# Threshold attention and gMLP on one core: transposes of two chunks at a time, loads one per step, value blocks in plain order

## The chip, the cores and the metric

The kernel runs on one core of one Trainium2 chip. Time is device microseconds (us) of one execution; several runs of one kernel are given by their median. The engines are PE (matrix multiply), DVE (vector), ACT (activation functions), POOL (GpSimd) and SP (here only an issuer of DMAs); each works through its own instructions in program order.

## What is computed

Attention with a threshold over 8 batches of 8 heads, 576 positions and 64 columns per head, and behind it a gMLP (spatial gating unit) on the joined heads.

```python
scores = (1/8) * q @ k.T
scores = where(scores >= max(scores) - tau, scores, -1e9)       # per row
attn   = exp(scores - max) ; attn /= sum(attn)
x      = (attn @ v)            # heads joined: (8, 576, 512)
h      = relu(x @ w_in)        # (8, 576, 1024)
u, v   = h[..., :512], h[..., 512:]
v_n    = (v - mean(v)) / sqrt(var(v) + 1e-6)
v_s    = einsum('ts,bsd->btd', w_spatial, v_n) + b_spatial[:, None]
out    = (u * v_s) @ w_out     # (8, 576, 512)
```

## The kernel before

Two heads of one batch are a pair; the 32 pairs are 32 slots of five steps. Step `c` of a slot takes one chunk of queries: chunks 0 to 3 are 128 queries of each of the two heads against 576 keys (1152 columns), chunk 4 is the last 64 queries of both heads. A step (`step`, L446 on) does this: PE computes the scores into one of two PSUM tiles `s` of three banks (L415, L418), DVE takes the row maximum `negm` (L460), ACT the exponential `e` (L468). One step later `mask` (L429) lets DVE set to zero what is under the threshold and write bf16 (`p`, L434; `pr` for chunk 4, L440), and SP issues a DMA that transposes the result SBUF to SBUF (`pT`, L437; `ptr` in two halves, L443 and L444), since the product with the values wants the keys on the partitions. That product, `pv` (L232), runs one slot later: head 0 of slot i in step 3 of slot i+1, head 1 in step 4. PE goes through chunk 0, 1, 2, 3 (from `pT`) and then chunk 4 (from `ptr`) in 25 small matmuls (L245), DVE normalises (`r`, `xn`, L254 and L255), and after head 1 one more DMA transpose makes `xT` (L260).

The work of the gMLP is cut into 20 jobs for each batch: five each of `moe_v`, `moe_u`, `moe_s`, `moe_o`. One is laid into each step, 27 steps behind the attention. So the `moe_v` jobs of a batch stand in steps 2, 3, 4 of slots 5, 9, 13, ... 29 and in steps 0, 1 of the slot after it, `moe_u` in the next five steps, and so on; each fourth slot has the same work. A `moe_v` job ends in a norm: ACT writes `vrel` with its sum (L297), POOL makes `nmean` of it (L299), ACT the squares `sq` (L305), POOL in turn `rs` (two instructions), `nm` and `vn` (L307 to L311). These jobs and `pv` share two PSUM banks `f`. For the last batch, which runs when the attention is over, the norm is made by DVE instead (L287 to L293), with one POOL instruction in it, and `uT` by DVE (L339).

In steps 0, 1, 2 of a slot PE also transposes q and k of the next pair (`qk_main`, `qk_rem`). What they read was loaded some slots ahead: in step 0 of every odd slot up to 27, SP issues nine loads for two pairs (L111 and L114 for q and k, L122 to L129 for v), all in one place, and POOL reshapes them (`shape_v` in step 0, L155; `shape_qk` in step 1, L146 and L149). The order on each engine is the order in which the program is written. At the start of slot 0, in step 3, `load_weights` issues the weights, the spatial matrix `wsl` from SP.

The lines that set the place of the loads, and of the first transposes behind them:

```python
                if c == 1 and slot + 2 < NPAIR:
                    shape_qk(slot + 2)
                if c == 0:
                    shape_v(slot)
                if c == 0 and slot % 2 and slot + 3 < NPAIR:
                    load_qk(slot + 3, 2)
                    load_v(slot + 3)
            ...
            step(i, c, fs[0] if fs else None, fs[1] if len(fs) > 1 else None)
```

Of the kernel before, what the change touches and what calls it, by code (L numbers as in the profile page):

```python
# [17 lines left out]
def kernel(  # L18
# [16 lines left out]

# [7 lines left out]
    P = 128  # L43
# [23 lines left out]
    NP_ = 3  # L67
    p_ring = [const.tile([P, 1152], BF16, name=f"p{i}") for i in range(NP_)]
    pr_ring = [const.tile([P, 704], BF16, name=f"pr{i}") for i in range(2)]
    v_ring = [const.tile([P, 10, D + 1], BF16, name=f"v{i}") for i in range(4)]  # L70
# [29 lines left out]
    wsl = const.tile([P, 5, S], F32, name="wsl")  # L100
    brow = const.tile([1, S], F32, name="brow")

    def load_qk(i, n):

        b, hp = divmod(i, HP)
        for t, src in zip(ld_ring[i // 2 % 2], (q, k)):
            t = t[:, 2 * (i % 2):2 * (i % 2) + 2 * n]
            src = src[b, 2 * hp:2 * hp + 2 * n]  # L110
# [6 lines left out]
    def load_v(i):  # L117
        b, hp = divmod(i, HP)
        vv = ld_ring[i // 2 % 2][2].rearrange("p (j h) c d -> p j (h c) d", h=2)
        va = v[b, 2 * hp:2 * hp + 4].rearrange("(j h) s d -> h j s d", h=2)  # L120
        fold = "j (p c) d -> p j (c d)"
        nc.sync.dma_start(out=vv[:, :, 0:4, :], in_=va[0, :, 0:512, :].rearrange(fold, c=4))  # L122
        nc.sync.dma_start(out=vv[0:64, :, 4, :],
                          in_=va[0, :, 512:576, :].rearrange("j p d -> p j d"))
# [4 lines left out]
        nc.sync.dma_start(out=vv[64:128, :, 9, :],  # L129
                          in_=va[1, :, 512:576, :].rearrange("j p d -> p j d"))  # L130
# [22 lines left out]
    def shape_v(i):  # L153
        j = i % 2
        nc.gpsimd.tensor_copy(  # L155
            out=v_ring[i % 4][:, :, 0:D],
            in_=ld_ring[i // 2 % 2][2][:, 2 * j:2 * j + 2].rearrange("p h c d -> p (h c) d"))


    def load_weights():  # L160
# [9 lines left out]
        nc.sync.dma_start(out=wsl[:, 0:4, :],  # L170
                          in_=moe_w_spatial[0:512, :].rearrange("(p c) s -> p c s", c=4))
        nc.sync.dma_start(out=wsl[0:64, 4, :], in_=moe_w_spatial[512:576, :])

    def shape_ws(c):
        n = P if c < 4 else 64
        nc.gpsimd.tensor_copy(
            out=wsb[:n, c, 0:512].rearrange("p (sc sp) -> p sc sp", sc=4),
            in_=wsl[:n, c, 0:512].rearrange("p (sp sc) -> p sc sp", sc=4))
        nc.gpsimd.tensor_copy(out=wsb[:n, c, 512:576], in_=wsl[:n, c, 512:576])
        nc.sync.dma_start_transpose(out=wsT[:, :, c * P:(c + 1) * P], in_=wsb[:, c, :])  # L180

    def shape_bias():
# [9 lines left out]
        nc.gpsimd.tensor_tensor(out=r2, in0=r1, in1=mid, op=ALU.subtract)
        nc.gpsimd.tensor_copy(out=lo, in_=r2)
        for n, t in enumerate((hi, mid, lo)):
            nc.sync.dma_start(out=wsT[64 + n:65 + n, 4, 0:S], in_=t[0:1, :])
# [367 lines left out]
```

## Time and profile before

| | |
|---|---|
| three runs | 627.15, 624.07, 620.58 us; median 624.07 |
| the profiled execution | 627.79 us |
| its span, first to last instruction | 625.7 us |
| PE matmul busy | 502.8 us (80% of the span) |
| DVE busy | 471.1 us (75%) |
| ACT, POOL busy | 327.9 us (52%), 223.1 us (36%) |
| SP's DMA queue, share of 16 DMA engines | 69.5% |
| mean granted TensorE clock | 0.918 |

Busy time counts every instruction from start to end, and neighbours on PE and DVE overlap a little, so an engine that shows 97% in a stretch is full there. The profile names for each engine what ended its idle times (the waits), follows back the chain of work that ended last, and gives for each DMA the time from issue to landing. The timeline gives start and length of each instruction; a bracket at its end is the idle time of its engine before it and what ended it.

### The profile page before, as it was taken

Reading aid. Unit: us, or ns where it says so; the run is one execution under the profiler, and the core shown is the slowest. Engines: PE = TensorE matmul, PEld = TensorE weight load, DVE = VectorE, ACT = ScalarE, POOL = GpSimd, SP = SyncE. Lnnn points to the kernel's source line nnn. Section 1 sums busy time; section 2 is a strip of 40 time slices with the busy share of each in tenths; the row PEclk is TensorE's granted clock in tenths of the full one; section 3 lists DMA queues with packets and bytes.
Section 4 is the critical chain, followed back from the end, with each engine's and each line's share of the span. In section 5 each row is a group of like instructions: output and inputs, shape, how many; then the busy total and the mean of one; then the engine's idle time right before and its main releaser. Section 6 shows DMA issues by size and latency. Waiting matters only on the chain.

```text
span 625.7 us, 10432 instructions
## 1 busy us (share of the span) xinstructions
PE 502.8 (80%) x3790; PEld 264.4 (42%) x3840; DVE 471.1 (75%) x516; ACT 327.9 (52%) x605; POOL 223.1 (36%) x398
## 2 busy tenths in 40 slices
PE   4725758688998989787997879787997879979756
PEld 2313334344544445343554435444554435535323
DVE  0835869788996879687896879677895869969463
ACT  1612435575475636575376726675375735765211
POOL 6527212373215522373116522364115622261010
PEclk9976879899997989899898989899897979989979
DMA  7799696948597687968698676957697585835502
GB/s 199 121 192 198 120 196 112 200 82 192 92 232 135 123 171 147 191 115 182 91 214 151 126 158 152 207 93 169 113 208 154 93 182 78 193 73 104 145 1 75
DMA packets 244930, 90.41 MB, mean 145 GB/s; under 512 B 214480, under 2 KB 239568, under 8 KB 244752
## 3 DMA queue, kind: packets, MB, share of 16 engines
q1 hardware_dynamic: 243744, 88.17, 69.5%
q0 software_dynamic: 1136, 1.58, 1.7%
q8 instruction: 30, 0.49, 0.3%
q14 instruction: 20, 0.16, 0.1%
HBM read 32.79 MB, written 9.44 MB: 67 GB/s over the span
## 4 chain that ended last, share of the span: by engine, by line
PE 36%; DVE 23%; DMA 15%; issue 8%; POOL 7%; ACT 6%; SPq 4%; POOLq 0%; ACTq 0%; DVEq 0%
PE s L415 14%; DVE p L434 10%; DVE negm L460 9%; DMA ptr<-pr 8%; PE f L245 6%; PE f L358 5%; DMA kl<-in_k_dram 3%; DMA wsl<-in_moe_w_spatial_dram 3%; PE f L324 2%; PE f L275 2%; ACT e L468 2%; ACT sq L305 2%; PE s L418 2%; PE f L388 2%; PE f L208 2%
## 5 line engine op out<-in xcount | busy, mean ns | idle before, releaser
L468 ACT ACTIVATE e<-s,negm 128x576 f32<-128x576 f32 x288 | 199.5, 739 | 135.7 <-DVE negm L460 127.7
L460 DVE TENSOR_REDUCE negm<-s 128x2 f32<-128x1152 f32 (+1 forms) x160 | 197.3, 1233 | 60.8 <-PE s L415 60.0
L434 DVE SCALAR_TENSOR_TENSOR p<-e,ctau 128x1152 bf16<-128x1152 f32 x128 | 189.2, 1478 | 13.2 <-DMA pT<-p 11.7
L415 PE MATMUL s<-qkT 64*128 64x512 f32 (+1 forms) x768 | 198.1, 611 | 1.2 <-ACT e L468 1.0
L229 POOL COPY kd<-qkT 64x64 f32<-64x64 f32 x32 | 7.4, 231 | 243.9 <-ACT qkT L225 224.0
L415 PEld LDWEIGHTS s<-qkT 64*128 64x128 f32 (+1 forms) x768 | 58.2, 181 | 35.1 <-issue 12.5
L212 ACT COPY qkT<-f 128x512 f32<-128x512 f32 x64 | 37.5, 586 | 63.8 <-PE f L208 63.8
L245 PEld LDWEIGHTS <-pT 128*128 128x128 bf16 x1280 | 51.6, 103 | 45.5 <-issue 23.1
L245 PE MATMUL f<-v,ptr 128*128 128x65 bf16 x320 | 22.7, 207 | 59.0 <-DMA ptr<-pr 59.0
L245 PE MATMUL f<-v,pT 128*128 128x65 bf16 x1280 | 56.2, 201 | 15.0 <-DMA pT<-p 10.4
L418 PE MATMUL s<-kd,qkT 128*128 128x128 f32 x256 | 55.8, 301 | 9.2 <-ACT e L468 6.9
L418 PEld LDWEIGHTS s<-kd,qkT 128*128 128x128 f32 x256 | 45.3, 197 | 25.0 <-ACT e L468 8.3
L254 DVE RECIPROCAL r<-f 128x5 f32<-128x5 f32 x64 | 12.2, 190 | 56.6 <-PE f L245 56.1
L146 POOL TENSOR_SCALAR qn<-ql 128x640 f32<-128x640 f32 x32 | 47.7, 1489 | 3.0 <-DMA ql<-in_q_dram 2.8
L275 PE MATMUL f<-w_in,xT 128*128 128x512 bf16 x145 | 43.8, 408 | 4.5 <-issue 1.3
L358 PE MATMUL f<-wsT,vn 128*128 128x512 bf16 x145 | 44.6, 429 | 2.9 <-ACT uT L344 1.0
L324 PE MATMUL f<-xT,w_in 128*128 128x512 bf16 x121 | 34.1, 396 | 13.0 <-ACT vrel L297 5.6
L388 PE MATMUL f<-w_o,gT 128*128 128x512 bf16 (+1 forms) x147 | 40.0, 379 | 2.7 <-DVE gT L375 1.3
L245 PEld LDWEIGHTS <-ptr 128*128 128x128 bf16 x320 | 16.1, 105 | 60.6 <-DMA ptr<-pr 56.0
L297 ACT ACTIVATE vrel<-f 128x512 f32<-128x512 f32 x35 | 20.8, 595 | 29.7 <-PE f L275 29.3
L396 ACT COPY o<-f 128x512 f32<-128x512 f32 (+1 forms) x38 | 22.2, 583 | 24.1 <-PE f L388 22.3
L255 DVE TENSOR_TENSOR xn<-f,r 128x320 bf16<-128x320 f32 x64 | 31.5, 491 | 2.2
(76 smaller groups left out, 489.3 us busy)
## 6 DMA issues: line engine op xcount, KB each, us to landing
out_dram<-o SPq DMA_DIRECT2D x32, 256.0 KB, 2.9
ql<-in_q_dram SPq DMA_DIRECT2D x15, 512.0 KB, 4.6
kl<-in_k_dram SPq DMA_DIRECT2D x15, 512.0 KB, 5.6
vl<-in_v_dram SPq DMA_DIRECT2D x16, 256.0 KB, 5.7
vl<-in_v_dram SPq DMA_DIRECT2D x32, 128.0 KB, 4.8
pT<-p SPq DMA_TRANSPOSE x128, 3.3
wsl<-in_moe_w_spatial_dram SPq DMA_DIRECT2D x1, 1152.0 KB, 18.3
vl<-in_v_dram SPq DMA_DIRECT2D x32, 32.0 KB, 4.9
```

What stands on the lines that cost most here:

```text
L146: nc.gpsimd.tensor_scalar(out=t, in0=src, scalar1=scale, scalar2=0.0, op0=ALU.mult, op1=ALU.add)
L212: nc.scalar.copy(out=qks[i][:, which, 0:512], in_=hold["t"])
L245: nc.tensor.matmul(out=t[:, c * 65:c * 65 + 65], lhsT=pts[i, c][:, blk, lo:lo + P], rhs=vt[:, 5 * h + j, :], start=(j == 0), stop=(j == 4))
L275: nc.tensor.matmul(out=t, lhsT=xts[b][:, f, c * P:(c + 1) * P], rhs=w_in[:, f, 512:1024], start=(f == 0), stop=(f == 3))
L324: nc.tensor.matmul(out=t, lhsT=w_in[:, m, f * P:(f + 1) * P], rhs=xts[b][:, m, 0:512], start=(m == 0), stop=(m == 3))
L358: nc.tensor.matmul(out=t, lhsT=vn[:, c, f * P:(f + 1) * P], rhs=wsT[:, c, 0:512], start=(c == 0), stop=(c == 4))
L388: nc.tensor.matmul(out=t[:n], lhsT=gs[b][:, f, c * P:c * P + n], rhs=w_o[:, f, :], start=(f == 0), stop=(f == 3))
L415: return nc.tensor.matmul(out=out, lhsT=qk[hs, 0, m], rhs=qk[hs, 1, lo:lo + n], start=True, stop=True)
L418: nc.tensor.matmul(out=view(s, 512, [[448, 2], [1, 64]]), lhsT=qk[:, 0, c * P:(c + 1) * P], rhs=kd_ring[i % 2], start=True, stop=True)
L434: nc.vector.scalar_tensor_tensor(out=pt, in0=ef, scalar=ctau, in1=ef, op0=ALU.is_ge, op1=ALU.mult)
L460: nc.vector.tensor_reduce(out=nm[:, 0:nh], in_=s, axis=AX.X, op=ALU.max, negate=True)
L468: nc.scalar.activation(out=e[:, h, :], in_=s[:, h, :], func=ACT.Exp, bias=nm[:, h:h + 1])
```

## The change

- `mask` writes chunks 0 and 1 into one tile, 2 and 3 into another, and issues one DMA transpose for each two chunks (18 blocks of 128x128, before 9); chunk 4 is transposed by one DMA of 5 blocks instead of two of 5 half blocks. `pv` indexes the new tiles. The value blocks of head 1 stay in plain order, with one extra block `vx` for the last 64 positions, which has its own small load and POOL copy (L147 of the changed kernel).
- The loads go into a queue, seven for two pairs (v in three instead of five), and one of them is issued at the head of each step; two per step in the first five.
- `shape_qk` stands in step 2 instead of step 1.
- `wsl` is loaded in three parts into tiles that the gMLP uses later.
- When the scores are over, the gMLP's jobs take their PSUM bank in turn from the two banks `f` and from the two score tiles. `uT` of the last batch is made by ACT. Its norm is put on the list `later`.

```diff
+    def load(i, n, w):
...
+        t = ld_ring[i // 2 % 2][w][:, 2 * (i % 2):2 * (i % 2) + 2 * n]
+        src = (q, k, v)[w][b, 2 * hp:2 * hp + 2 * n]
+        def main():
             nc.sync.dma_start(
                 out=t[:, :, 0:4, :],
                 in_=src[:, 0:512, :].rearrange("h (p c) d -> p h (c d)", c=4))
+        def rest():
             nc.sync.dma_start(out=t[0:64, :, 4, :],
                               in_=src[:, 512:576, :].rearrange("h p d -> p h d"))
...
+        def rest_b():
+            nc.sync.dma_start(
+                out=vx_ring[i // 2 % 2][64:128],
+                in_=src.rearrange("(j h) s d -> h s j d", h=2)[1, 512:576])
+        return [main, rest] + ([rest_b] if w == 2 else [])
...
+    def bank():
+        banks[0] += 1
+        if "scores" in done_with and banks[0] % 2:
+            return ps_s.tile([P, 1536], F32, name="s")[:, 0:512]
+        return ps_f.tile([P, 512], F32, name="f")
...
                 for j in range(5):
-                    blk = 4 + j if (h == 1 and c < 4) else j
-                    lo = 64 if (h == 1 and c == 4) else 0
...
+                    if c < 4:
+                        lhs = pts[i, c // 2][:, c % 2, 4 + (j + 1) % 5 if h else j, :]
+                        rhs = vt[:, (10 if j == 4 else 5 + j) if h else j, :]
+                    else:
+                        lhs = pts[i, 2][:, j, 64 * h:64 * h + P]
+                        rhs = vt[:, 5 * h + j, :]
...
                 nc.gpsimd.tensor_tensor(out=rs, in0=rs, in1=mhalf, op=ALU.pow)
-                nc.vector.tensor_scalar(out=dst, in0=vrel[:n], scalar1=mv[:n, 0:1],
-                                        scalar2=rs[:n], op0=ALU.subtract, op1=ALU.mult)
+                def norm():
+                    nc.vector.tensor_scalar(out=dst, in0=vrel[:n], scalar1=mv[:n, 0:1],
+                                            scalar2=rs[:n], op0=ALU.subtract, op1=ALU.mult)
+                later.append(norm)
...
-            if f < 4 and b == B - 1:
-                nc.vector.tensor_scalar(out=us[b][:, f, 0:512], in0=t, scalar1=0.0, scalar2=0.0,
-                                        op0=ALU.max, op1=ALU.add)
-            elif f < 4:
+            if f < 4:
                 nc.scalar.activation(out=us[b][:, f, 0:512], in_=t, func=ACT.Relu)
...
-            pt = p_ring[(i * 4 + c) % NP_]
+            pt = p_ring[c // 2]
...
-            dst = ptp.tile([P, 9, P], BF16, name="pT")
-            nc.sync.dma_start_transpose(out=dst, in_=pt)
+            if c % 2:
+                dst = ptp.tile([P, 2, 9, P], BF16, name="pT")
+                nc.sync.dma_start_transpose(out=dst.rearrange("p c b s -> p (c b) s"),
+                                            in_=pt.rearrange("p c s -> p (c s)"))
+                pts[i, c // 2] = dst
...
-            dst = ptr_ring[i % 3]
-            nc.sync.dma_start_transpose(out=dst[:, :, 0:64], in_=pt[0:64, 64:704])
-            nc.sync.dma_start_transpose(out=dst[:, :, 64:128], in_=pt[64:128, 0:640])
+            pts[i, 2] = ptr_ring[i % 3]
+            nc.sync.dma_start_transpose(out=pts[i, 2][:, :, 0:P], in_=pt)
...
-                if c == 1 and slot + 2 < NPAIR:
+                if c == 2 and slot + 2 < NPAIR:
                     shape_qk(slot + 2)
...
-                if c == 0 and slot % 2 and slot + 3 < NPAIR:
-                    load_qk(slot + 3, 2)
-                    load_v(slot + 3)
+                if c == 0 and slot % 2 and slot + 3 < NPAIR or g == 0:
+                    for w in range(3):
+                        queue.extend(load(slot + (3 if g else 2), 2, w))
...
+            else:
+                done_with.add("scores")
...
+            for f in queue[:1 if g > 4 else 2]:
+                queue.pop(0)()
             step(i, c, fs[0] if fs else None, fs[1] if len(fs) > 1 else None)
```

SP, around step 0 of an odd slot in the steady part: `xT` of the slot before closes step 4 of the even slot, then come the odd slot's loads and `ptr`. Before:

```order
L437 DMA_TRANSPOSE pT<-p_104 128x9x128
L260 DMA_TRANSPOSE xT<-xn 128x5x128
L111 DMA ql_116<-in_q_dram 128x4x256
L114 DMA ql_116<-in_q_dram 64x4x64
L111 DMA kl_117<-in_k_dram 128x4x256
L114 DMA kl_117<-in_k_dram 64x4x64
L122 DMA vl_118<-in_v_dram 128x2x256
L123 DMA vl_118<-in_v_dram 64x2x64
L125 DMA vl_118<-in_v_dram 64x2x256
L127 DMA vl_118<-in_v_dram 64x2x256
```

Behind these stand the ninth load and then the two halves of `ptr`. Of the change:

```order
L438 DMA_TRANSPOSE pT<-p_103 128x18x128
L264 DMA_TRANSPOSE xT<-xn 128x5x128
L107 DMA ql_115<-in_q_dram 128x4x256
L446 DMA_TRANSPOSE ptr_150<-pr_104 128x5x128
L112 DMA ql_115<-in_q_dram 64x4x64
L107 DMA kl_116<-in_k_dram 128x4x256
L438 DMA_TRANSPOSE pT<-p_102 128x18x128
L112 DMA kl_116<-in_k_dram 64x4x64
L107 DMA vl_117<-in_v_dram 128x4x256
L264 DMA_TRANSPOSE xT<-xn 128x5x128
L438 DMA_TRANSPOSE pT<-p_103 128x18x128
```

One load instead of nine now stands between `xT` and `ptr`; the others stand behind `ptr`, the load of v ahead of the slot's second `pT`.

POOL, where the norm of the third `moe_v` job (`nmean`, step 4 of slots 5, 9, ...) is followed by the slot after it. Before:

```order
L299 TENSOR_SCALAR nmean<-sm 128x1
L307 TENSOR_SCALAR rs<-ss 128x1
L309 TENSOR_TENSOR rs<-rs,mhalf 128x1
L310 TENSOR_TENSOR nm<-nmean,rs 128x1
L311 TENSOR_SCALAR vn_111<-vrel,rs,nm 128x512
L155 CAST v_109<-vl_118 128x10x64
L146 TENSOR_SCALAR qn<-ql_113 128x640
L149 COPY kn<-kl_114 128x640
L299 TENSOR_SCALAR nmean<-sm 128x1
```

Of the change:

```order
L305 TENSOR_SCALAR nmean<-sm 128x1
L313 TENSOR_SCALAR rs<-ss 128x1
L315 TENSOR_TENSOR rs<-rs,mhalf 128x1
L316 TENSOR_TENSOR nm<-nmean,rs 128x1
L317 TENSOR_SCALAR vn_110<-vrel,rs,nm 128x512
L144 CAST v_108<-vl_117 128x10x64
L147 CAST v_108<-vx_125 128x64
L305 TENSOR_SCALAR nmean<-sm 128x1
```

The reshaping of q and k has gone from ahead of the fourth `nmean` to behind that job's norm, and one small copy has come in; the first three norms stand as they stood.

DVE, the last norm of the last batch and what follows it. Before:

```order
L287 BN_STATS st<-vrel 128x6
L289 BN_AGGR mv<-st 128x2
L290 TENSOR_SCALAR rs<-mv 128x1
L293 TENSOR_SCALAR vn_112<-vrel,mv,rs 64x512
L339 TENSOR_SCALAR uT<-f 128x512 x4
L372 TENSOR_TENSOR gT<-f,uT 128x512 x4
```

Of the change:

```order
L290 BN_STATS st<-vrel 128x6
L292 BN_AGGR mv<-st 128x2
L293 TENSOR_SCALAR rs<-mv 128x1
L298 TENSOR_SCALAR vn_111<-vrel,mv,rs 64x512
L373 TENSOR_TENSOR gT<-s,uT 128x512
L373 TENSOR_TENSOR gT<-f,uT 128x512
```

The four `uT` have left DVE; `vn` stands where it stood, behind the statistics of its own job, since `later` is emptied in the same step.

## Rows read from the trace of the kernel before

**Rows 1.** Busy time by stretch: span, five engines, clock, DMA share, GB/s.

```profile
295.00:301.00 6.00, 5.19 (x29) 2.20 (x30) 3.17 (x5) 0.00 (x0) 0.00 (x0) 0.50 0.79 146
301.50:319.00 17.50, 17.18 (x151) 9.57 (x151) 16.94 (x21) 9.86 (x16) 3.64 (x5) 1.00 0.70 126
```

**Rows 2.** Waits: engine and line, what for, us in total, times, longest.

```profile
PE f L245 <- DMA ptr<-pr: 59.0, 16, 7.3
```

**Rows 3.** Timeline of SP, slots 14 and 15: start, us, what.

```profile
281.99 1.87 SPq L437 DMA_TRANSPOSE pT<-p  x1
...
285.62 0.39 SPq L111 DMA_DIRECT2D ql<-in_q_dram  x1
...
291.40 1.24 SPq L443 DMA_TRANSPOSE ptr<-pr  x1
292.68 1.24 SPq L444 DMA_TRANSPOSE ptr<-pr  x1
```

**Rows 4.** Timeline of PE, step 3 of slot 15.

```profile
295.81 0.43 PE L245 MATMUL f<-v,ptr 128*128 128x65 bf16 x5 [3.71 <-DMA ptr<-pr]
```

**Rows 5.** Timeline of DVE: the first negm of slots 9, 14 to 17, 29 to 31, and others.

```profile
176.73 1.36 DVE L460 TENSOR_REDUCE negm<-s 128x2 f32<-128x1152 f32 x1
...
266.81 1.36 DVE L460 TENSOR_REDUCE negm<-s 128x2 f32<-128x1152 f32 x1 [0.65 <-PE s L415]
...
282.95 1.36 DVE L460 TENSOR_REDUCE negm<-s 128x2 f32<-128x1152 f32 x1 [0.40 <-PE s L415]
284.23 0.81 DVE L440 SCALAR_TENSOR_TENSOR pr<-e,ctau 128x576 bf16<-128x576 f32 x1
...
292.08 1.34 DVE L460 TENSOR_REDUCE negm<-s 128x2 f32<-128x1152 f32 x1
...
304.44 1.35 DVE L460 TENSOR_REDUCE negm<-s 128x2 f32<-128x1152 f32 x1
...
318.71 1.36 DVE L460 TENSOR_REDUCE negm<-s 128x2 f32<-128x1152 f32 x1
...
533.47 1.36 DVE L460 TENSOR_REDUCE negm<-s 128x2 f32<-128x1152 f32 x1
...
548.07 1.36 DVE L460 TENSOR_REDUCE negm<-s 128x2 f32<-128x1152 f32 x1 [0.17 <-PE s L415]
...
567.36 1.35 DVE L460 TENSOR_REDUCE negm<-s 128x2 f32<-128x1152 f32 x1
...
575.40 1.35 DVE L460 TENSOR_REDUCE negm<-s 128x2 f32<-128x1152 f32 x1
...
579.22 0.75 DVE L460 TENSOR_REDUCE negm<-s 128x1 f32<-128x576 f32 x1
```

**Rows 6.** Timeline of POOL and ACT at the start of slot 30.

```profile
550.77 0.19 POOL L299 TENSOR_SCALAR nmean<-sm 128x1 f32<-128x1 f32 x1
...
550.99 0.72 ACT L305 ACTIVATE sq<-vrel,nmean 128x512 bf16<-128x512 f32 x1 [3.58 <-POOL nmean L299]
```

**Rows 7.** DMA issues by line: count, KB each, median us from issue to landing.

```profile
ql<-in_q_dram SPq DMA_DIRECT2D x15, 512.0 KB, 4.6
pT<-p SPq DMA_TRANSPOSE x128, 3.3
xT<-xn SPq DMA_TRANSPOSE x32, 2.6
```

**Rows 8.** Timeline of PE in slot 1, the first product with values.

```profile
45.74 0.46 PE L245 MATMUL f<-v,pT 128*128 128x65 bf16 x5 [0.50 <-DMA pT<-p]
53.55 0.44 PE L245 MATMUL f<-v,ptr 128*128 128x65 bf16 x5 [7.35 <-DMA ptr<-pr]
```

**Rows 9.** Timeline of the last batch's gMLP: PE and DVE.

```profile
604.94 0.54 DVE L293 TENSOR_SCALAR vn<-vrel,mv,rs 64x512 bf16<-64x512 f32 x1 [0.66 <-POOL rs L292]
...
606.13 3.57 PE L324 MATMUL f<-xT,w_in 128*128 128x512 bf16 x8 [5.50 <-DVE uT L339]
...
610.49 5.27 PE L358 MATMUL f<-wsT,vn 128*128 128x512 bf16 x19
```

More of the change, by code (lines that the diff above doesn't have):

```diff
@@ L65 @@
     nc.vector.memset(mhalf, -0.5)
[L67 to L70, printed above, removed]
+    p_ring = [const.tile([P, 2, 1152], BF16, name=f"p{i}") for i in range(2)]
+    pr_ring = [const.tile([P, 640], BF16, name=f"pr{i}") for i in range(2)]
+    v_ring = [const.tile([P, 11, D + 1], BF16, name=f"v{i}") for i in range(4)]
     vn_ring = [const.tile([P, 5, 512], BF16, name=f"vn{i}") for i in range(2)]
@@ L74 @@
     for ts in ld_ring:
-        for t in ts[:2]:
+        for t in ts:
             nc.gpsimd.memset(t[64:128, :, 4, :], 0.0)
-        vv = ts[2].rearrange("p (j h) c d -> p j (h c) d", h=2)
-        nc.gpsimd.memset(vv[64:128, :, 4, :], 0.0)
-        nc.gpsimd.memset(vv[0:64, :, 5, :], 0.0)
+    vx_ring = [const.tile([P, 2, D], F32, name=f"vx{i}") for i in range(2)]
+    for t in vx_ring:
+        nc.gpsimd.memset(t[0:64], 0.0)
     kd_ring = [const.tile([P, P], F32, name=f"kd{i}") for i in range(2)]
@@ L155, in shape_v @@
         nc.gpsimd.tensor_copy(
-            out=v_ring[i % 4][:, :, 0:D],
+            out=v_ring[i % 4][:, 0:10, 0:D],
             in_=ld_ring[i // 2 % 2][2][:, 2 * j:2 * j + 2].rearrange("p h c d -> p (h c) d"))
+        nc.gpsimd.tensor_copy(out=v_ring[i % 4][:, 10, 0:D], in_=vx_ring[i // 2 % 2][:, j, :])
+    parts = const.tile([1, 3, S], BF16, name="parts")
+    wsl = [mw.tile([P, 2, S], F32, name=n) for n in ("uT", "uT", "gT")]
+    bias = mw.tile([P, 2, S], F32, name="gT")
     def load_weights():
@@ L168, in load_weights @@
         nc.gpsimd.memset(wsb[:, :, S:640], 0.0)
         nc.gpsimd.memset(wsb[64:128, 4, :], 0.0)
[L170 to L172 removed]
+        for j in range(2):
+            nc.sync.dma_start(out=wsl[j], in_=moe_w_spatial[0:512, :].rearrange(
+                "(p c) s -> p c s", c=4)[:, 2 * j:2 * j + 2, :])
+        nc.sync.dma_start(out=wsl[2][0:64, 0, :], in_=moe_w_spatial[512:576, :])
@@ L192, in shape_bias @@
[L192 to L195, printed above, removed]
+        b32, r32 = bias[0:1, 0, :], bias[0:1, 1, :]
+        nc.gpsimd.tensor_copy(out=parts[:, 0, :], in_=b32)
+        nc.gpsimd.tensor_tensor(out=r32, in0=b32, in1=parts[:, 0, :], op=ALU.subtract)
+        nc.gpsimd.tensor_copy(out=parts[:, 1, :], in_=r32)
@@ new lines, in shape_bias @@
+        nc.gpsimd.tensor_tensor(out=b32, in0=r32, in1=parts[:, 1, :], op=ALU.subtract)
+        nc.gpsimd.tensor_copy(out=parts[:, 2, :], in_=b32)
+        for n in range(3):
+            nc.sync.dma_start(out=wsT[64 + n:65 + n, 4, 0:S], in_=parts[:, n, :])
+    banks = [0]
+    def bank():
[3 more added lines that the diff above has]
+        return ps_f.tile([P, 512], F32, name="f")
+    done_with = set()
@@ L489 @@
     with tc.manual_schedule():
-        load_qk(0, 1)
+        for w in (0, 1):
+            for f in load(0, 1, w):
+                f()
         shape_qk(0)
@@ L494 @@
             f[2]()
-        load_qk(1, 1)
+        for w in (0, 1):
+            for f in load(1, 1, w):
+                f()
         shape_qk(1)
-        load_v(0)
-        load_qk(2, 2)
-        load_v(2)
+        for f in load(0, 2, 2):
+            f()
+        queue = []
         for g in range(20 * B + LAG):
```

82 lines of the change are left out of this document (24 added, 58 removed).

## The prediction

> **What bounds the kernel now.** I read the waits first. In them one line stands out on PE: it waits 59.0 us in 16 places for `ptr`, the transposed chunk 4 [rows 2]. The timeline then shows where. In slot 15 DVE has finished `pr` at 284.23 + 0.81 = 285.04 [rows 5], but SP issues its two transposes only at 291.40 and 292.68 [rows 3], because the nine loads of that odd slot stand ahead of them on SP, from 285.62 on. PE, in the middle of `pv`, stops at 292.10 and goes on at 295.81 [rows 4]. Behind such a pause the granted clock was 0.50, the lower of the two levels (1.2 of 2.4 GHz), for the six us that followed [rows 1], so that the step costs more than the pause.
>
> What the kernel could do without it is seen by the distance between the first `negm` of one slot and of the next [rows 5]. Slots of the same work recur every four, so I name them by their number modulo 4. Slot 16 (type 0, no loads) took 318.71 - 304.44 = 14.27 us, and in it PE and DVE were busy 17.18 and 16.94 of 17.50 us [rows 1]: two engines are full there, and nothing of this change makes them shorter. Slot 14 (type 2) took 282.95 - 266.81 = 16.14, slot 15 (type 3, loaded) 304.44 - 282.95 = 21.49. Slots 9 to 28 took (533.47 - 176.73) / 5 = 71.35 for each four. Less 14.27 and 16.14, that leaves 40.94 for the two odd, loaded ones.
>
> Slot 29 is the experiment that the trace brings along: type 1, but nothing is left to load. It took 548.07 - 533.47 = 14.60. And slot 30 behind it shows what is late next: 567.36 - 548.07 = 19.29 instead of 16.14. ACT there stood 3.58 us for the third `nmean` [rows 6]. POOL works in order and has the whole norms of the first two `moe_v` jobs ahead of that `nmean`; ACT, also in order, holds the copies of q and the exponentials behind its `sq`. In the loaded slots of type 1, PE's pause for `ptr` falls just there and gives POOL the time.
>
> **The change, part by part.**
>
> *Loads in a queue, one transpose for chunk 4.* SP has one load (0.39 us of issue in [rows 3]) between `xT` and `ptr` instead of nine. `ptr` can then be issued at about 286 instead of 291.4, and there is one instead of two. Its shape is that of `xT`, which lands after 2.6 us [rows 7]: about 288.6, and PE wants it at 292.10. For the upper bound I let it start only when the load of q ahead of it has landed: 285.62 + 4.6 + 2.6 = 292.8, 0.7 us too late. The nearest row for `ptr` behind loads is slot 15 itself: its second half was issued at 292.68 behind all nine and let PE go on at 295.81, 3.1 us later, so 2.6 to 3.1 is nearer than 7.2. I take no wait, bounds 0 and 0.7 us in 13 slots, 9 us.
>
> The Trainium skill (DMA: Bandwidth & Descriptors, Queues, rings and completion order) says that on each DMA engine descriptors of one queue are consumed in ring order. That speaks against the change: an earlier issue alone wins nothing if the load's data goes first. Taken strictly it is the upper bound above.
>
> *What a loaded slot then costs.* Type 1: 14.60, as slot 29. Type 3: steps 0 to 2 as they are in slot 15, 292.08 - 282.95 = 9.13; step 3 as in slot 31, which had no loads, 579.22 - 575.40 = 3.82; step 4 the same with half the row maximum, 0.75 instead of 1.35, so 3.22. Together 16.17. The two cost 30.77 instead of 40.94, 5.1 us less each. Loaded slots in the steady part are 3, 5, ... 27, thirteen: 13 x 5.1 = **66 us** less.
>
> *What is late next.* The third `nmean` keeps its place on POOL. So slots 6, 10, ... 26 become like slot 30: 6 x (19.29 - 16.14) = **19 us** more. Slot 30 has it already. The moved `shape_qk` leaves the space before the fourth `nmean` and goes ahead of the fifth; in slot 30 there is no `shape_qk` at all and the wait was there, so I give the move nothing. Its bounds are 0 and a gain of the whole wait (rival A).
>
> *Transposes of two chunks.* 5 blocks land after 2.6 us, 9 after 3.3 [rows 7], so 18 should land after about 3.3 + 9 x 0.175 = 4.9; the upper bound is two whole ones in a row, 6.6. The last chunk's transpose of slot 14 was issued at 281.99 [rows 3], and PE came to the end of it some 10 us later, at 292.10. Both bounds are hidden by that. With the load of v ahead of it on SP (4.6 us for a like load of q) the sum of the bounds is 11.2, but that is in the odd slots only, and by the nearer values 4.9 and part of 4.6 it is hidden. The tiles `p` are written again four steps later, about 11 us, so DVE doesn't wait for them. SP has three transposes a slot fewer, which frees only SP. I take nothing.
>
> *Value blocks, `vx`.* The matmuls are as many as before. One small POOL copy is added in each slot, hidden in POOL's idle time, which is 64% of the span; without that cover it would add to the wait of rows 6.
>
> *The start.* In slot 1 the transposes wait behind the weights in the DMA engines. PE got the last `pT` at 45.74 and `ptr` only at 53.55 [rows 8], again behind nine loads. `pT` I leave where it is, since as many bytes are in front of it; `ptr` behind one load should come some 2 us after it: **6 us** less. Bounds 3 (the larger transposes are later by one landing) and 7.8 (with `pT`).
>
> *The end.* `vn` stays behind its own statistics on DVE, so putting it on `later` delays nothing and brings nothing: the chain of five norms ends at 604.94 + 0.54 = 605.48 as before [rows 9]. But `uT` no longer stands behind it. PE waited 5.50 us for it, ran `moe_u` from 606.13 and began `moe_s` at 610.49. With four banks and ACT, `moe_u` is done while the norms run, and `moe_s` begins at 605.5, 5.0 us earlier. PE has then stood idle for about as long, so that the slow six us as in [rows 1] fall on `moe_s` instead of `moe_u`; some 4.4 us more of it run at half speed, which gives back 2.2. **2.8 us** less, bounds 0 and 5.
>
> **Sum.** 66 - 19 + 6 + 3 = 56 us. The profiled execution took 627.8, so 572; it was the longest of the three runs, and against the median of 624.1 it is **568 us**.
>
> **Rivals.**
>
> A. *POOL's wait doesn't come back.* For it: slots 10 to 26 take 16.14 as long as PE is held up a little before them, and a rest of the wait for `ptr` of 1 or 2 us would be hidden there. Against it: slot 30, where nothing else was late. Then 568 - 19 = 549.
>
> B. *`ptr` stays late by about half*, because the load of q and the pair of chunks ahead of it fill the DMA engines (their share was 0.79 in the stretch behind the loads, [rows 1]). Half of 66 is lost, and with it half of the 19 isn't paid: 568 + 33 - 9 = 592. Against it: the 3.1 us above.
>
> C. *The pair's transpose lands late, and the kernel gets slower.* The trace has no transpose of 18 blocks. If it took 13 us and more, PE would pause in every slot for 3.7 us as it now does in the odd ones: instead of 66 less, 17 more slots at 5.1, so 624 + 87 - 9 = about 702. It decides from the point at which each slot waits long enough to eat the gain of 56 / 32 = 1.75 us, a landing of about 12 us, over three times that of 9 blocks. The step from 5 to 9 blocks speaks against it.
>
> D. *The wait only moves* to another engine in the same slots, for instance to POOL or ACT, and the time stays within 1%, about 622. Slot 29 speaks against it, which had all the other work and took 14.60.
>
> **How the numbers follow.** The forecast 0.55, A 0.2, B 0.13, C 0.05, D 0.07. A measurement of this kernel can tell about 1% from no change. Faster by more: 0.55 + 0.2 + 0.13 = 0.88; the same 0.07; slower 0.05. The range takes in A and B and the bounds: low 549 less 4 for the end and the start, 545; high 592 plus 9 for `ptr`, 601.
>
> **What would show it.** Right: no wait of PE for `ptr` above 1 us from slot 3 on; slots of type 1 at about 14.6 and of type 3 at about 16.2; ACT's `sq` waiting over 3 us for `nmean` once in each fourth slot, with slots of type 2 at about 19.3; a landing of `pT` near 4.9 us; `moe_s` of the last batch beginning right behind the last `vn`. Wrong: PE waiting for `pT` in the even slots (C), for `ptr` in the odd ones (B), slots of type 2 still at 16.1 (A).

## The result, and the profile after

The changed kernel takes 583.9 us (median of 4 runs, 582.2 to 587.2), the kernel before 625.4 us (4 runs): a ratio of 0.935 with a 95% interval of 0.928 to 0.943. That is faster and inside the range, but 16 us above the predicted 568. The profiled executions differ by 627.8 - 585.4 = 42.4 us, where 56 were forecast; their spans, 625.7 and 583.6 us, by 42 us.

Cut at the first `negm` of each slot, the span falls apart like this:

| stretch | before | after | difference | forecast |
|---|---|---|---|---|
| slots 0 to 2 | 61.0 | 57.8 | -3.2 | -6 |
| the 13 loaded slots 3, 5, ... 27 | 262.0 | 197.0 | -65.0 | -66 |
| type 2: slots 6, 10, ... 26 | 96.8 | 126.7 | +29.9 | +19 |
| all others up to 30 | 133.0 | 133.2 | +0.2 | 0 |
| from slot 31 to the end | 58.3 | 54.4 | -3.9 | -2.8 |

So one term carries most of the error, 11 of 14 us: what came back in the slots of type 2. The start missed by 3 us more. The lines of after that answer to [rows 5], DVE's timeline, the first `negm` of slots 10, 11, 14, 15 and 16 (start, us, what):

```profile
178.65 1.36 DVE L461 TENSOR_REDUCE negm<-s 128x2 f32<-128x1152 f32 x1 [0.16 <-PE s L415]
...
198.67 1.35 DVE L461 TENSOR_REDUCE negm<-s 128x2 f32<-128x1152 f32 x1
...
243.71 1.36 DVE L461 TENSOR_REDUCE negm<-s 128x2 f32<-128x1152 f32 x1 [0.21 <-PE s L415]
...
266.04 1.36 DVE L461 TENSOR_REDUCE negm<-s 128x2 f32<-128x1152 f32 x1 [0.40 <-PE s L415]
...
282.19 1.35 DVE L461 TENSOR_REDUCE negm<-s 128x2 f32<-128x1152 f32 x1
```

Slot 15, loaded, took 282.19 - 266.04 = 16.15 us (21.49 before, 16.17 forecast). Slot 10 took 20.02 and slot 14 took 22.33, where 19.29 was forecast and 16.14 was the time before.

The waits of after, which answer to [rows 2] (engine and line, what for, us in total, times, longest):

```profile
ACT sq L311 <- POOL nmean L305: 33.9, 14, 3.8
PE f L250 <- DMA pT<-p: 20.4, 6, 6.3
...
PE f L250 <- DMA ptr<-pr: 6.0, 4, 2.4
```

PE's 59.0 us for `ptr` have become 6.0, and from slot 3 on none is over 1 us. ACT's wait for `nmean`, 10.4 us before, is now the largest of the three. PE's waits for `pT` have risen from 10.4 to 20.4 us: two in slot 1, one each in slots 2, 4 and 31, and a sixth, of 3.2 us in slot 26. That one belongs to ACT's wait for `nmean`: PE goes on 1.34 us behind `sq`, as it does in slot 14 below, and a `pT` happened to land just then.

Why `ptr` is in time: SP's timeline in slot 15 (start, us of issue, what), against [rows 3],

```profile
269.91 0.54 SPq L107 DMA_DIRECT2D ql<-in_q_dram  x1
270.54 1.23 SPq L446 DMA_TRANSPOSE ptr<-pr  x1
```

and the DMAs issued from 264 to 283 us, by line (count, KB each, median us from issue to landing):

```profile
ql<-in_q_dram SPq DMA_DIRECT2D x1, 512.0 KB, 4.5
...
ptr<-pr SPq DMA_TRANSPOSE x1, 4.5
```

`ptr` is issued right behind one load and lands at 275.04, 0.6 us after that load (274.41). PE takes it at 275.09 without a wait. So it is with all 14 `ptr` that are issued right behind a load of q: each lands 0.6 to 0.9 us after the load. The rule of the Trainium skill that the prediction weighed (DMA: Bandwidth & Descriptors, Queues, rings and completion order) is one of the order in which descriptors are taken, not of the order of landing. The trace shows landings alone, and they fit it: in all 14 the earlier load came home first. Its cost is hidden, but the margin in slot 15 was 0.05 us.

Now the term that failed. In slot 10 ACT waits for the third `nmean`, as forecast from [rows 6], and behind it PE runs at the lower of its clock's two levels (0.50, 1.2 of 2.4 GHz). ACT's timeline, PE's timeline, and the busy time by stretch (columns as in rows 1):

```profile
181.56 0.72 ACT L311 ACTIVATE sq<-vrel,nmean 128x512 bf16<-128x512 f32 x1 [3.57 <-POOL nmean L305]
```

```profile
184.75 1.86 PE L278 MATMUL f<-w_in,xT 128*128 128x512 bf16 x4 [1.20 <-ACT vrel L303]
...
186.97 2.08 PE L415 MATMUL s<-qkT 64*128 64x512 f32 x4
```

```profile
184.00:187.00 3.00, 2.25 (x8) 1.11 (x7) 1.47 (x1) 2.88 (x7) 2.53 (x4) 0.50 0.89 197
```

In slot 14 the same wait (3.62 us) leaves the clock at 1.00, step 1 is 2 us shorter (5.7 against 7.7 us), and then there is a second wait in the same slot, for the fifth `nmean`. By stretch, and on POOL, ACT and PE:

```profile
252.00:255.00 3.00, 2.42 (x14) 1.24 (x12) 2.69 (x2) 2.54 (x7) 2.20 (x4) 1.00 0.35 67
```

```profile
253.72 1.76 POOL L317 TENSOR_SCALAR vn<-vrel,rs,nm 128x512 bf16<-128x512 f32 x1
255.46 0.72 POOL L135 TENSOR_SCALAR qn<-ql 128x640 f32<-128x640 f32 x1
256.12 0.71 POOL L138 COPY kn<-kl 128x640 f32<-128x640 f32 x1
256.81 1.35 POOL L305 TENSOR_SCALAR nmean<-sm 128x1 f32<-128x1 f32 x1
```

```profile
258.19 0.72 ACT L311 ACTIVATE sq<-vrel,nmean 128x512 bf16<-128x512 f32 x1 [3.26 <-POOL nmean L305]
```

```profile
259.53 1.26 PE L250 MATMUL f<-v,pT 128*128 128x65 bf16 x20 [3.19 <-ACT uT L344]
```

`qn` and `kn`, the moved `shape_qk`, now stand between the norm of the fourth job and the `nmean` of the fifth. ACT's `sq`, behind it the two `uT`, and behind those PE's `pv` wait for them. Slot 26 has the same chain (the same 3.26 us on ACT) and took 23.83 us.

### The profile page after: what moved, and what is told of

It is laid out like the page before. It is cut to its first block, busy times and chain, and to the rows that moved or that the text cites. A ratio compares the mean times of both kernels' runs of the same rounds, so it can differ in the third digit from the quotient of the medians.

```text
span 583.6 us, 10239 instructions
## 1 busy us (share of the span) xinstructions
PE 495.0 (85%) x3840; PEld 260.3 (45%) x3840; DVE 462.5 (79%) x512; ACT 328.6 (56%) x609; POOL 242.2 (42%) x432
## 4 chain that ended last, share of the span: by engine, by line
DVE 31%; PE 27%; POOL 16%; issue 10%; ACT 9%; DMA 6%; SPq 1%; POOLq 0%; ACTq 0%; DVEq 0%
DVE p L434 13%; DVE negm L461 11%; PE s L415 10%; POOL vn L317 4%; PE f L250 4%; ACT sq L311 3%; ACT e L469 3%; PE f L329 3%; POOL rs L315 3%; DMA ptr<-pr 2%; DVE gT L373 2%; PE f L278 2%; PE f L359 2%; DVE xn L259 2%; PE s L418 2%
## 5 line engine op out<-in xcount | busy, mean ns | idle before, releaser
L415 PE MATMUL s<-qkT 64*128 64x512 f32 (+1 forms) x768 | 191.9, 592 | 1.0 <-ACT e L469 1.0
L250 PE MATMUL f<-v,pT 128*128 128x65 bf16 x1280 | 55.3, 199 | 26.2 <-DMA pT<-p 20.4
L415 PEld LDWEIGHTS s<-qkT 64*128 64x128 f32 (+1 forms) x768 | 56.4, 175 | 30.4 <-issue 6.9
L278 PE MATMUL f<-w_in,xT 128*128 128x512 bf16 x148 | 41.6, 406 | 8.7 <-ACT vrel L303 8.4
L311 ACT ACTIVATE sq<-vrel,nmean 128x512 bf16<-128x512 f32 x35 | 25.1, 721 | 34.7 <-POOL nmean L305 33.9
L359 PE MATMUL f<-wsT,vn 128*128 128x512 bf16 x150 | 37.9, 384 | 5.6 <-DVE gT L373 4.0
L138 POOL COPY kn<-kl 128x640 f32<-128x640 f32 x32 | 25.3, 791 | 40.8 <-DMA kl<-in_k_dram 40.8
L388 PE MATMUL f<-w_o,gT 128*128 128x512 bf16 (+1 forms) x140 | 36.1, 380 | 2.1 <-DVE gT L376 1.3
L317 POOL TENSOR_SCALAR vn<-vrel,rs,nm 128x512 bf16<-128x512 f32 (+1 forms) x35 | 33.1, 947 | 3.8
L396 ACT COPY o<-f 128x512 f32<-128x512 f32 (+1 forms) x35 | 20.4, 583 | 22.9 <-PE f L388 21.2
L135 POOL TENSOR_SCALAR qn<-ql 128x640 f32<-128x640 f32 x32 | 28.7, 898 | 8.9 <-DMA ql<-in_q_dram 4.9
```

The source lines that it names most:

```text
L250: nc.tensor.matmul(out=t[:, c * 65:c * 65 + 65], lhsT=lhs, rhs=rhs, start=(j == 0), stop=(j == 4))
L278: nc.tensor.matmul(out=t, lhsT=xts[b][:, f, c * P:(c + 1) * P], rhs=w_in[:, f, 512:1024], start=(f == 0), stop=(f == 3))
L311: nc.scalar.activation(out=sq, in_=vrel, func=ACT.Square, bias=nmean, accum_out=ss)
L317: nc.gpsimd.tensor_scalar(out=dst, in0=vrel[:n], scalar1=rs[:n], scalar2=nm[:n], op0=ALU.mult, op1=ALU.add)
L359: nc.tensor.matmul(out=t, lhsT=vn[:, c, f * P:(f + 1) * P], rhs=wsT[:, c, 0:512], start=(c == 0), stop=(c == 4))
L415: return nc.tensor.matmul(out=out, lhsT=qk[hs, 0, m], rhs=qk[hs, 1, lo:lo + n], start=True, stop=True)
```

## The experiments

All eleven kernels were timed beside the kernel before, and the ratios are to that. "Type 2" are slots 6, 10, ... 26, together.

**The moved `shape_qk`, taken back in the changed kernel.** (In slot 0 it stays in step 2.)

```diff
-                if c == 2 and slot + 2 < NPAIR:
+                if c == (2 if slot == 0 else 1) and slot + 2 < NPAIR:
```

> The changed kernel with shape_qk back in step 1 (in slot 0 it stays in step 2, where its loads stand ahead of it). Theory: the prediction took the move of shape_qk for free, but in the changed kernel it stands ahead of the fifth nmean, and slots of type 2 take 20.0 to 23.8 us instead of the 19.3 of slot 30 before; the second wait of ACT for nmean, in slots 14 and 26, is its doing. Then these slots come down to 19.3 to 20, the second wait is gone, the first (3.6 us, third nmean) stays, and the time falls by 6 to 11 us, to 573 to 578. Rival: the excess is from the pair transposes or from vx; then type 2 stays at 20 to 24 and the time at 584.

581.3 us, ratio 0.931 (0.926 to 0.935): hardly to be told from the changed kernel, and less than expected. Type 2 is 4.1 us shorter, at 20.0 to 21.3 each. ACT's timeline in slot 14 shows where the rest went:

```profile
246.60 0.72 ACT L311 ACTIVATE sq<-vrel,nmean 128x512 bf16<-128x512 f32 x1 [3.57 <-POOL nmean L305]
...
252.96 0.72 ACT L311 ACTIVATE sq<-vrel,nmean 128x512 bf16<-128x512 f32 x1 [1.47 <-POOL nmean L305]
...
256.84 0.72 ACT L311 ACTIVATE sq<-vrel,nmean 128x512 bf16<-128x512 f32 x1 [1.07 <-POOL nmean L305]
```

The wait has moved back to the fourth `nmean`, with a rest at the fifth. POOL is behind by more than one place in the order can mend.

**`nmean` on ACT.**

```diff
-            nc.gpsimd.tensor_scalar(out=nmean, in0=sm, scalar1=-1.0 / 512, scalar2=0.0,
-                                    op0=ALU.mult, op1=ALU.add)
+            nc.scalar.activation(out=nmean, in_=sm, func=ACT.Copy, scale=-1.0 / 512)
```

> The changed kernel with nmean made by ACT (a copy with a scale) instead of POOL; the rest of the norm stays on POOL. Theory: in slots of type 2 ACT waits for nmean only because POOL has two whole norms ahead of it. Then ACT's wait for nmean is gone, type 2 falls to about 16.1 as long as nothing else is late, 6 slots by 5 us and slot 30 by 2.4, so about 32 us less: 552. Rival: what is late in these slots is POOL as a whole (vn, the copies) or ACT with its 35 more instructions; then type 2 stays above 18.5 and the time above 570.

547.8 us, ratio 0.878 (0.875 to 0.881), 36 us less than the changed kernel for one instruction of one column. ACT and DVE at slot 10, and a stretch of that slot:

```profile
173.02 0.20 ACT L305 ACTIVATE nmean<-sm 128x1 f32<-128x1 f32 x1
...
173.75 0.71 ACT L310 ACTIVATE sq<-vrel,nmean 128x512 bf16<-128x512 f32 x1
```

```profile
173.99 1.36 DVE L460 TENSOR_REDUCE negm<-s 128x2 f32<-128x1152 f32 x1 [0.16 <-PE s L414]
...
189.31 1.35 DVE L460 TENSOR_REDUCE negm<-s 128x2 f32<-128x1152 f32 x1
```

```profile
182.00:185.00 3.00, 3.00 (x36) 1.71 (x37) 2.25 (x3) 2.56 (x6) 2.73 (x6) 1.00 0.54 102
```

`sq` follows its own `nmean` and waits for nobody, the clock stays at 1.00, and the slot takes 15.32 us. Type 2 together is 92.3 us, 34.4 less than in the changed kernel and even 4.6 less than before. So ACT's wait for POOL is the whole of the 29.9 us, both kinds of slot included.

**Transposes of one chunk, as before** (nine tiles `pT`, three `p`; chunk 4 still by one DMA).

```diff
-            pt = p_ring[c // 2]
+            pt = p_ring[(i * 4 + c) % 3]
...
-            if c % 2:
-                dst = ptp.tile([P, 2, 9, P], BF16, name="pT")
...
+            dst = ptp.tile([P, 9, P], BF16, name="pT")
+            nc.sync.dma_start_transpose(out=dst, in_=pt)
+            pts[i, c] = dst
```

> The changed kernel with each chunk transposed by its own DMA, as before (9 blocks each, three tiles p, nine of pT); all the rest stays. Theory: the pair brings nothing in the steady part, since PE does not wait for pT there; in slot 2, where PE waited 3.3 us for the second pair, something may be won: 579 to 586. Rival 1: fewer transposes were part of the gain; then single ones bring waits for ptr or pT back and the time is 595 or more. Rival 2: SP held for 3.3 us by each pair costs in each slot; then the time is under 575.

578.2 us, ratio 0.928 (0.923 to 0.933). Loaded slots are as in the changed kernel, type 2 is 20.0 to 20.1 except slot 6 with 22.3, and slots 1 and 2 together take 45.7 (45.0 with pairs). The transposes of two chunks bring nothing. Of what they cost here, 6 us by the medians, 4.2 us lie in type 2 in the profiled executions: the second wait fell in one slot instead of two. Another 2.5 us lie behind the first `negm` of slot 31 (51.9 against 54.4 us). There PE waits for the last chunks of the attention, in the changed kernel and in this one:

```profile
549.20 0.73 PE L250 MATMUL f<-v,pT 128*128 128x65 bf16 x10 [2.56 <-DMA pT<-p]
```

```profile
542.44 0.33 PE L250 MATMUL f<-v,pT 128*128 128x65 bf16 x5 [1.16 <-DMA pT<-p]
```

**All seven loads in step 0 again.**

```diff
-            for f in queue[:1 if g > 4 else 2]:
+            for f in queue[:7 if g > 4 else 2]:
```

> The changed kernel with all seven loads of two pairs issued in step 0 of the odd slot instead of one per step (the first ones as in the change). Theory: the place of the loads ahead of ptr made the wait; seven at 0.6 us are 4.2 us ahead of ptr, 3.7 more than now, and ptr had 2 to 3 us to spare: PE waits 1 to 2 us for ptr in each of 13 slots, followed by the lower clock, and the loaded slots get longer by 1.5 to 3; part of it is hidden by the wait for nmean: 595 to 610. Rival: one transpose for ptr instead of two was enough; then the time stays at 584.

650.1 us, ratio 1.043 (1.039 to 1.048): slower than the kernel before. The waits have the old line again:

```profile
PE f L250 <- DMA ptr<-pr: 54.8, 14, 7.0
```

The loaded slots take 265.3 us (262.0 before, 197.0 in the changed kernel): the place of the loads is the 65 us, shown both ways. The single `ptr`, which this kernel keeps, wins nothing there by itself. But type 2 takes 123.1 us as well, although here the pause for `ptr` gives POOL its time: in all six slots ACT waits 3.49 us for the fifth `nmean`. Something else in the change costs 26 us under these conditions. The next run has it alone.

**The kernel before, with `shape_qk` in step 2 and nothing else.**

```diff
-                if c == 1 and slot + 2 < NPAIR:
+                if c == 2 and slot + 2 < NPAIR:
```

> The kernel before with one edit alone: shape_qk in step 2 instead of step 1. Theory 1 (the move is a loss by itself: qn and kn now stand on POOL ahead of the fifth nmean, and ACT, PE behind it, waits for that): slots 6, 10, ... 26 go from 16.1 to about 20, as in the kernel with all loads in one place, so 6 x 4 = 24 us more, about 649 us. Theory 2 (my prediction's: the move is free, and the long slots of that kernel come from its other edits): slots of 16.1, about 625 us.

643.7 us, ratio 1.033 (1.027 to 1.040). Slot 10 on DVE (its first `negm` and that of slot 11), POOL, ACT and PE:

```profile
197.63 1.36 DVE L460 TENSOR_REDUCE negm<-s 128x2 f32<-128x1152 f32 x1 [0.93 <-PE s L415]
...
218.87 1.36 DVE L460 TENSOR_REDUCE negm<-s 128x2 f32<-128x1152 f32 x1 [0.65 <-PE s L415]
```

```profile
206.94 0.72 POOL L146 TENSOR_SCALAR qn<-ql 128x640 f32<-128x640 f32 x1
207.61 0.72 POOL L149 COPY kn<-kl 128x640 f32<-128x640 f32 x1
208.29 1.30 POOL L299 TENSOR_SCALAR nmean<-sm 128x1 f32<-128x1 f32 x1
```

```profile
209.62 0.72 ACT L305 ACTIVATE sq<-vrel,nmean 128x512 bf16<-128x512 f32 x1 [3.49 <-POOL nmean L299]
```

```profile
210.97 1.26 PE L245 MATMUL f<-v,pT 128*128 128x65 bf16 x20 [3.25 <-ACT uT L342]
```

Slot 10 takes 21.24 us instead of 16.14, all of type 2 122.0 instead of 96.8: 25 us for moving 1.4 us of POOL's work by one step. In four of the six slots the lower clock followed the wait (0.69 to 0.71 granted in step 3, slots of 21.1 to 21.3 us); in slots 6 and 22 it stayed at 1.00, and they take 18.58. The loaded slots gave 10.5 back (251.5 instead of 262.0), in an execution of 639.1 us, the fastest of the four. By the medians the edit costs 21 us. The edit that the prediction priced at nothing is a loss by itself. In the changed kernel it shows in full in slots 14 and 26 alone; in the other four the wait for the third `nmean` and the lower clock behind it come first, and 0.2 to 0.7 us are left at the fifth.

**The kernel before, with `nmean` on ACT and nothing else** (the edit is that shown above).

> The kernel before with one edit alone: nmean is made by ACT instead of POOL, the edit that took 36 us from the changed kernel. Theory 1 (before the change the wait for nmean lay in the shade of the wait for ptr): only slot 30, which has no ptr wait ahead of it, gains, from 19.3 to 15.5, and the slots 6 to 26 stay at about 16: 4 us less, about 621 us; PE's wait for ptr stays near 59 us. Theory 2 (it is a cost of its own): about 590 us.

613.5 us, ratio 0.985 (0.981 to 0.989), between the two theories and nearer the first. Slot 30 goes from 19.29 to 15.51 as expected, and type 2 from 16.14 to 15.0 to 15.2, 5.8 us together, which I had not expected: a rest of the wait, 1.0 us for the fifth `nmean`, stood in those slots already. The wait for `ptr` is unmoved:

```profile
PE f L245 <- DMA ptr<-pr: 58.4, 17, 7.4
```

So the same edit is worth 9 us ahead of the change and 36 behind it.

**Without the pairs and the moved `shape_qk`:** the changed kernel with transposes of one chunk and `shape_qk` in step 1 (both edits as above). The spread loads and the one transpose for chunk 4 stay, and so do the value blocks, the `wsl` in three parts and the end.

> The changed kernel with two of its parts taken back: transposes of one chunk each and shape_qk in step 1 again; what stays are the loads spread one per step, the single transpose of chunk 4, and the end. Theory 1 (the loads' place is the whole gain, and the wait for the third nmean is its one follow-up): loaded slots of 14.6 and 16.2, slots 6 to 26 of 20.0 to 20.3 with no second wait in them, about 576 us, not more than 3 us from the kernel with single transposes alone. Theory 2 (with shape_qk back in step 1 the wait moves to the fourth nmean, as in the run with that edit alone, and slots of type 2 stay above 20.5 in places): 578 to 581 us.

577.6 us, ratio 0.925 (0.920 to 0.929). Type 2 is 19.9 to 20.5 in all six slots, 120.8 together. The clock fell behind the first wait in all six (0.66 to 0.77 granted in step 1), and none has the second wait of 3.26 us; but ACT waits 1.5 us for the fourth `nmean` in each and 0.75 for the fifth in three, so the wait of Theory 2 is there, only shorter. The pairs and the moved `shape_qk` thus have no part in the gain. The loaded slots take 198.1 us, 64 less than before, by the place of the loads with the single `ptr`; spread loads with `ptr` still in two halves were not run.

**`nmean` on ACT, with transposes of one chunk.**

> The changed kernel with nmean on ACT and the transposes taken back to one chunk each, ptr still one DMA. Theory 1 (the transposes of two chunks neither bring nor cost anything once no norm waits on POOL; what single ones won in the run before, 6 us, was only the chance of where the second wait fell): 547 us, within 2 us of the kernel with nmean on ACT alone. Theory 2 (the longer issue and the later landing of the pairs cost by themselves): 542 us or less. Theory 3 (the pairs are a gain, since SP issues less): 551 us or more.

544.6 us, ratio 0.874 (0.871 to 0.878), against 0.878 (0.875 to 0.881) with pairs: the intervals overlap, and nearly all steady slots agree within 0.02 us (16.15, 14.27, 14.58 and 15.32 in both). There Theory 1 holds. From slot 31 on it takes 51.7 us against 53.1 with pairs: PE waits 1.32 us for the last `pT` instead of 2.86. So the pairs do cost something, at the end.

**`nmean` on ACT, with `shape_qk` back in step 1.**

> The changed kernel with nmean on ACT and shape_qk back in step 1. Theory 1 (shape_qk hurts only where a norm waits behind it on POOL for its nmean): slots of type 2 of 15.3 as with nmean on ACT alone, 547 us, within 2 us of it. Theory 2 (qn and kn in step 1 hold up rs and vn, or in step 2 the transposes of q and k, whoever makes nmean): 3 us or more off, slots of type 2 at other lengths.

547.1 us, ratio 0.875 (0.871 to 0.879): no difference to `nmean` on ACT alone, type 2 of 15.17. The place of `shape_qk` matters only while an `nmean` stands behind it.

**`nmean` on ACT, with the gMLP in the two banks `f` to the end.**

```diff
-        if "scores" in done_with and banks[0] % 2:
+        if False:
```

> The changed kernel with nmean on ACT, and with the gMLP's jobs kept in the two banks f to the end, as before the change (uT still by ACT). Theory 1 (two of the four banks are what lets moe_u run while the last norms are made): the last moe_u and moe_s come some 2 to 4 us later, about 551 us. Theory 2 (uT on ACT alone does it): 548 us, as with four banks.

547.0 us, ratio 0.878 (0.874 to 0.881): no difference. With two banks the last `vn` starts at 531.39, with four at 531.35, in spans of 545.3 and 544.9 us. The four banks bring nothing, which leaves `uT` on ACT; that edit was not run by itself.

**The norms of the last batch really one step later** (with `nmean` on ACT and transposes of one chunk).

```diff
-                later.append(norm)
+                norms.append(norm)
...
         later.clear()
+        later.extend(norms)
+        norms.clear()
```

> The changed kernel with nmean on ACT, transposes of one chunk, and the last batch's norms put on a list of their own, so that each vn really stands one step later on DVE, behind the statistics of the next job. Theory 1 (the chain of five norms at the end, 2.2 us each of which 0.66 is a wait for POOL's rs, sets the end): DVE's waits for rs go, 4 x 0.66 = 2.6 us less than the kernel with nmean on ACT and single transposes, 542 us. Theory 2 (moe_s only waits somewhere else, for gT or for uT): no difference, 544.6 us.

540.5 us (6 runs, 539.6 to 542.0), ratio 0.865 (0.862 to 0.868): 4 us less than without it, and the fastest kernel of this study. DVE's timeline:

```profile
520.02 0.54 DVE L299 TENSOR_SCALAR vn<-vrel,mv,rs 128x512 bf16<-128x512 f32 x1
520.47 0.69 DVE L291 BATCH_NORM_STATS2 st<-vrel 128x6 f32<-128x512 f32 x1
...
525.38 0.54 DVE L299 TENSOR_SCALAR vn<-vrel,mv,rs 64x512 bf16<-64x512 f32 x1 [0.44 <-POOL rs L296]
```

Four of the five waits for `rs`, 0.66 us each [rows 9], are gone, and from the first statistics to the last `vn` it is 8.1 us instead of 11.3.

## Why the prediction was right, and where it was wrong

**The loaded slots: right.** The step rested on slot 29, which had the same work and no loads. 65.0 us measured, 66 forecast; from slot 7 on, type 1 14.6 to 15.1, type 3 16.1 to 16.2. Rivals B and D fell with the wait for `ptr`, and rival C with the waits for `pT`, of which slots 5 to 27 have none of their own. Rival A fell with type 2: POOL's wait did come back.

**"What is late next": the right mechanism, the term mis-sized.** It was +19 and measured +29.9. Two parts can be told apart. The four slots without a long second wait take 20.1 on average, as do the six of the run without pairs and move, instead of the 19.29 of slot 30: that is 5 us in six slots. Slot 30 was a poor model, since it reshapes no q and k; that this is the reason is argued, not shown. The other 6 us are slots 14 and 26, with a second wait. That wait comes from the sentence "I give the move nothing": its bounds, 0 and a gain, left out a loss. Taking the move back recovers 4.1 of the 6 us. The reason given, that slot 30 has the wait without any `shape_qk`, speaks of the third `nmean` alone. It didn't ask which `nmean` the moved work would stand ahead of, and whether that one had slack. It has none, and the trace of before said so. There, in slot 14, ACT already waits for the fifth `nmean`, and PE behind it:

```profile
276.36 0.72 ACT L305 ACTIVATE sq<-vrel,nmean 128x512 bf16<-128x512 f32 x1 [0.99 <-POOL nmean L299]
```

```profile
277.71 0.80 PE L245 MATMUL f<-v,pT 128*128 128x65 bf16 x20 [0.44 <-ACT uT L342]
```

All six slots of type 2 have this wait, of 0.99 to 1.04 us. The move alone makes it 3.49, and these slots 25 us longer.

Why the clock held in slot 14 and fell in slot 10, behind waits of 3.62 and 3.57 us, stays open. It went with whether POOL caught up: at half clock PE's step 1 took 2 us longer, and the fifth `nmean` then came nearly in time. In the twelve slots of type 2 of this kernel and of that with transposes of one chunk, the long second wait stands in just the three in which the clock stayed at 1.00 through step 1 (14 and 26 here, 6 there); in the other nine it was 0.66 to 0.77. In which slots the second wait falls is therefore chance, as far as is known.

**Transposes of two chunks: nothing in the steady slots, as forecast, but a loss at the end.** They land after 5.6 us (median), between the 4.9 taken and the bound of 6.6, hidden in the steady slots. But the 10 us that were to hide them aren't there for the last pair: it is issued at 543.86, and PE, which has no scores left to compute, comes to it at 546.64. PE waits 2.3 to 3.0 us for it in the six kernels with pairs, 1.1 to 1.7 in the four changed ones without. The first statistics of the last batch begin 28.4 to 29.2 us behind the first `negm` of slot 31 with pairs, 25.8 to 26.1 without: a loss of 2.8 us on average, which the prediction put at nothing. "SP has three transposes a slot fewer, which frees only SP" is wrong. SP's issues of `pT`, before and then after (ns, least/median/most):

```profile
L437 SPq DMA_TRANSPOSE pT<-p x128: 1242/1302/9822, 20.6 to 582.0; - x128
```

```profile
L438 SPq DMA_TRANSPOSE pT<-p x64: 2457/3272/9034, 22.7 to 543.9; - x64
```

A pair occupies SP 2.5 times as long as one chunk. With the one `ptr` that is 2 x 3.27 + 1.23 = 7.8 us a slot, where it was 4 x 1.30 + 2 x 1.24 = 7.7 before [rows 3]. The margin of `ptr` shrinks with it: in slot 15 it lands 0.05 us ahead of PE with pairs, 1.84 us with transposes of one chunk.

**The start: half of it, and not by the working.** Slot 1 became 6.3 us shorter (32.22 to 25.97), as the working said. But slot 2 became 3.6 us longer, on PE:

```profile
63.31 0.49 PE L250 MATMUL f<-v,pT 128*128 128x65 bf16 x10 [3.27 <-DMA pT<-p]
66.20 0.46 PE L250 MATMUL f<-v,ptr 128*128 128x65 bf16 x5 [2.40 <-DMA ptr<-pr]
```

PE comes to slot 1's products earlier than SP can issue their transposes behind loads and `wsT`. It isn't the pairs: with single ones the two slots take as long. With all seven loads in step 0 the wait for `ptr` is back in slot 1, and it is slot 2 that is short (30.88 and 13.40 us):

```profile
51.29 0.46 PE L250 MATMUL f<-v,ptr 128*128 128x65 bf16 x5 [7.00 <-DMA ptr<-pr]
```

Together the two slots take 44.3 us so, and 45.0 with the loads spread: the place of the loads only moved the wait from one slot to the next. That both are below the 47.7 of before is then owed to some other part of the change, and which one was not tried.

**The end: 3.9 instead of 2.8, by two errors that offset each other.** The chain of norms didn't end as before: counted from the first `negm` of slot 31, the last `vn` ended at 39.7 us instead of 38.1, since the pairs came late. What follows it took 14.7 us instead of 20.2, so 5.5 less. That `vn` on `later` delays nothing was right, and the run that really delays it shows what the name of the edit promised: 4 us. "With four banks and ACT" was half wrong: the four banks have no part in it. PE in the changed kernel, against [rows 9]:

```profile
564.40 0.81 PE L359 MATMUL s<-wsT,vn 128*128 128x512 bf16 x3
566.80 0.39 PE L359 MATMUL s<-wsT,vn 128*128 128x512 bf16 x1 [1.59 <-DVE vn L298]
```

`moe_s` doesn't begin behind the last `vn`, as forecast, but takes the first three as they are there: 0.8 us of its work is done before the chain ends.

## What to carry to other kernels

When a wait is taken away, ask of every in-order engine what it had been catching up on in that pause; here a scalar of 0.19 us on POOL, queued behind whole norms, gave back almost half of a 65 us gain, and moving it to the engine that uses it brought 36 us. Before work is moved past an instruction, name the next instruction of that engine that somebody waits for, and look up its slack in the trace: here a wait of 1 us already stood there, and 1.4 us of moved work made the six slots 25 us longer. Work that is merged to save issues also comes later, and that shows where nothing is left to hide it, here at the end. A slot in the trace that happens to lack the disturbed work is the best model of what an edit leaves, but check what else it lacks.

## What the hardware showed that was not expected

POOL's small instructions stand still while DVE masks. The `nmean` of slot 14 above took 1.35 us, from 256.81 to 258.16; that of the job before took 0.19. On DVE, and on POOL:

```profile
256.69 1.41 DVE L434 SCALAR_TENSOR_TENSOR p<-e,ctau 128x1152 bf16<-128x1152 f32 x1
```

```profile
251.41 0.19 POOL L305 TENSOR_SCALAR nmean<-sm 128x1 f32<-128x1 f32 x1
```

DVE's `p` runs from 256.69 to 258.10, the long `nmean` ends 0.06 us behind it, and POOL's next instruction starts at 258.10. `vn` at 253.72 and the `nmean` of the run with `shape_qk` alone, at 208.29, are long in the same way. Of the 35 `nmean` in the trace of the changed kernel, the 12 that begin while DVE masks take 1.00 to 1.35 us, the other 23 0.18 to 0.19. The Trainium skill (SBUF — State Buffer, SBUF: two separate sides) says that a DVE operation with two SBUF inputs and a GpSimd operation that reads SBUF lock each other out for a whole instruction. `p` reads `e` from SBUF as both its inputs, and the trace agrees, with some 1.2 us more for a one-column instruction. A chain on POOL beside a busy DVE is therefore longer than the sum of its instructions' shortest times: in the run with `shape_qk` alone, ACT's wait grew by 2.5 us (0.99 to 3.49), of which `qn` and `kn` are 1.4 and the lengthened `nmean` 1.1.
